# A copy block moved ahead of two others on ScalarE, and weight conversions begun earlier, in a three-stage attention and MLP-mixer kernel

## The chip, the cores and the metric

The kernel runs on one core of a Trainium2 chip. The metric is the device time of one execution in microseconds (us), as the median of three runs. TensorE is called PE here, VectorE DVE, ScalarE ACT, GpSimd POOL, and SyncE SP; SP issues the DMAs of this kernel.

## The reference

Local attention with a few global columns, then two token/channel mixers. Cut to what matters:

```python
x = attention(q, k, v)                      # B=2, S=768, E=512
# first mixer
u = x + (relu(x^T @ w_tok1) @ w_tok2)^T
u = u + relu(u @ w_ch1) @ w_ch2             # w_ch1: 512 x 1536
# second mixer (moe2)
theta = x @ w_theta
zr, zi = x * cos(theta), x * sin(theta)
yr = einsum('ts,bsd->btd', w_tok_r, zr)
yi = einsum('ts,bsd->btd', w_tok_i, zi)
u = x + yr + yi
out = u + relu(u @ w_ch)
```

The weights are 64-bit floats. The kernel keeps each operand of these products as two float32r halves, a high one (the rounded value) and a low one (the rest), and multiplies three pairs of halves for each product (`mm3`: high by high, high by low, low by high, in this order).

## The kernel before

Everything is written out in order by hand; each engine works through its own queue of instructions in that order, and semaphores hold an instruction until its inputs are there. There are three parts: the attention, the channel product of the first mixer (`channel_mix`, two batches b of twelve chunks k each), and the second mixer (`PhaseB.run`).

**The late steps.** `PhaseB.run` loops over twelve blocks i of 128 rows. In step i PE does `mix(i, 0)` (24 products y <- z and wri, 256 columns), `theta(i + 2)` (12 products th), and `mix(i, 1)` and `mix(i, 2)` (12 products of 512 columns each). What the other engines do in step i serves later blocks:

- `rotate(i + 1)`: DVE multiplies x by sine and by cosine (line 1170, two instructions), ACT copies each result as the high half of z (line 1171), POOL subtracts to get the low halves (line 1173, two instructions) and adds the two halves of xt to get x again (line 1177). `mix(i + 1, 0)` needs both. The high halves are read by its first product, the low half of the cosine part by its third. z has two buffers, named s and z in the trace: even blocks are in s, odd blocks in z.
- `turn_in(i + 3)`: the block i + 3 was turned by a DMA a step earlier, as 16-bit halves in the tile cut_xt. ACT joins the halves (line 789), ACT copies the high half of xt (line 792), DVE subtracts to get the low half (line 793).
- `turn_out(i + 4)`: ACT cuts the next block into 16-bit halves (line 779) in the same tile cut_xt, and SP issues the DMA that turns it.
- `theta(i + 2)`: after the products th, DVE reduces the angle (lines 1139, 1142, 1143, 1146, 1147), and ACT takes one absolute value and two sines (lines 1150 to 1152) that `rotate(i + 2)` needs one step later.
- `tick`, twice in steps 0 to 3 and once in the others: the conversion of weight pieces from 64-bit words to two float32r halves. A piece passes four phases in four successive ticks: two ACT instructions (lines 139, 140), then DVE, DVE and POOL (lines 145, 148, 149), then ACT (line 157), then DVE (line 160). Each tick moves every piece that is under way on by one phase and then begins one new piece, if its gate is open. A gate is a number that a counter has to reach; the counter goes up once for each chunk of the second batch. `need` adds ticks where a piece is not yet done.

In the first batch of `channel_mix` there is a tick after each of the two halves h of a chunk, in the second batch only after h = 1, and one more after the chunk's second product for most k.

Of the kernel before, what the change touches and what calls it, by code (L numbers as in the profile page):

```python
# [20 lines left out]
ALU = mybir.AluOpType  # L21
# [43 lines left out]
def r(ap):  # L65
    return ap.bitcast(F32R)
# [17 lines left out]
class Build:  # L84
# [851 lines left out]
    def moe_jobs(self, ws, w12p):  # L936

        dram = self.dram
        self.start_jobs()
        self.wc_job, self.wr_job = {}, {}  # L940
        self.wt, self.wr, self.wch = [], [], []
        self.ws, self.w12p = ws, w12p

        for i in range(2 * NF):
            self.wc_job[divmod(i, 2)] = 0 if i < self.EARLY else self.channel_job(*divmod(i, 2))

        def theta(d):
            if d == 0:
                self.s0 = self.xs_rows(0, self.xs_raw(0, "s0"))
                self.s1_raw = self.xs_raw(1, "s1")  # L950
                self.s1 = self.xs_rows(1, self.s1_raw)
                for i in range(NE):
                    t = self.s0 if i < 3 else self.s1
                    j = 2 * (i % 3)
                    self.wt.append((t[:, j], t[:, j + 1]))
            return self.wt[d]

        for d in range(NE):
            self.wt_job = self.add_job(
                dram["w_theta"][d * P : (d + 1) * P, :], lambda d=d: theta(d), 1  # L960
            )

        def token(i):
            if i < self.EARLY:
                w = self.early.tile([P, 2, E], F32, name="wri%d" % i, tag="w")
            else:
                w = self.split_tile(i - self.EARLY, "wri%d" % i, True)
            self.wr.append((w[:, 0], w[:, 1]))
            return self.wr[i]

        for i in range(3 * NS):
            s, j = divmod(i, 3)
            self.wr_job[s] = self.add_job(
                dram["w_tok"][s * P : (s + 1) * P, 2 * j * E : 2 * (j + 1) * E],
                lambda i=i: token(i),
                2 + i // 2,
            )

        def last(d):
            if d == 0:  # L980
                raw = w12p.tile([P, NS * 2 * E + W12_PAD], F32, name="wch", tag="w")
                w = raw[:, 0 : NS * 2 * E].rearrange("p (a l e) -> p a l e", a=NS, l=2)
                self.wch = [(w[:, i, 0], w[:, i, 1]) for i in range(NE)]
                self.wch_rest = w[:, NE:NS].rearrange("p a l e -> p (a l) e")
                self.wch_late = raw[:, NE * 2 * E + SHIFT : NS * 2 * E + SHIFT]
            return self.wch[d]

        for d in range(NE):
            self.wch_job = self.add_job(
                dram["w_ch"][d * P : (d + 1) * P, :], lambda d=d: last(d), 1 + NF  # L990
            )
# [28 lines left out]
    def channel_mix(self, gp, pb):  # L1020
        nc = self.nc
        steps = [(b, k) for b in range(B) for k in range(NF)]
        ho = {}

        def up(b, k):
            self.need(self.wc_job[k, 0])
            c1 = self.wc[k][0]
            uth, utl = self.ut[b]
            g = gp.tile([P, 2, S], F32R, name="g_%d_%d" % (b, k), tag="g")
            for h, hs in enumerate((slice(0, E), slice(E, S))):  # L1030
                ps = self.ps.tile([P, hs.stop - hs.start], F32, name="gp_%d_%d_%d" % (b, k, h), tag="t")
                self.mm3(
                    ps,
                    [
                        ((r(c1[0][:, d]), r(c1[1][:, d])), (r(uth[h][:, d]), r(utl[h][:, d])))
                        for d in range(NE)
                    ],
                )
                self.evac_split(g[:, 0, hs], g[:, 1, hs], ps, relu=True)
                if b == 0 or h == 1:  # L1040
                    self.tick()
            return g

        def down(b, k, g):
            self.need(self.wc_job[k, 1])
            c2 = self.wc[k][1]
            if k == 0:
                ho[b] = [
                    self.ps.tile([P, E], F32, name="h2_%d_%d" % (b, s), tag="acc") for s in range(NS)
                ]  # L1050
            for s in range(NS):
                cs = slice(s * P, (s + 1) * P)
                self.mm3(
                    ho[b][s],
                    [((g[:, 0, cs], g[:, 1, cs]), (r(c2[0]), r(c2[1])))],
                    first=k == 0,
                    last=k == NF - 1,
                )
                if k == NF - 1:
                    x = self.x[b][:, s, :]  # L1060
                    nc.vector.tensor_tensor(out=x, in0=ho[b][s], in1=x, op=ALU.add)  # L1061

        g = up(*steps[0])
        self.turning = {}
        plan = {2: [(pb.turn_out, 0)], 3: [(pb.turn_in, 0), (pb.turn_out, 1)], 4: [(pb.turn_in, 1)],
                5: [(pb.theta, 0)], 6: [(pb.rotate, 0), (pb.turn_out, 2)], 7: [(pb.theta, 1)],
                8: [(pb.turn_in, 2)], 9: [(pb.turn_out, 3)]}
        for i, (b, k) in enumerate(steps):
            nxt = up(*steps[i + 1]) if i + 1 < len(steps) else None
            if b == 0:  # L1070
                if 0 <= k - 4 < NS:
                    self.columns_split(k - 4)
                if 0 <= k - 3 < NS:
                    self.halves_join(self.turning[k - 3], nc.gpsimd.tensor_copy)
                if 0 <= k - 2 < NS:
                    self.columns_out(pb, k - 2)
            if b == 1:
                for act, n in plan.get(k, ()):
                    act(n)
            down(b, k, g)  # L1080
            if b == 1 and k < NF - 1 and k not in (5, 6, 7):
                self.tick()
            if (b, k) == (0, NF - 2) or b == 1:
                self.gate += 1
            g = nxt
        pb.run()


class PhaseB:
# [21 lines left out]
    def turn_in(self, i):  # L1111

        K = self.k
        j = (2, 1, 0)[i % 3] if i > 2 else i % 2
        if j not in self.xtile:
            pool, tag = (self.tp, "t") if j == 2 else (self.xtp, "xt%d" % j)
            self.xtile[j] = pool.tile([P, 2, NE, P], F32, name="xt%d" % j, tag=tag)
        t = self.xt[i] = self.xtile[j]
        K.halves_join(self.cut, K.nc.scalar.copy)
        K.halves_split(self.cut, r(t[:, 0]), r(t[:, 1]))  # L1120

    def theta(self, i):
        K, nc = self.k, self.k.nc
# [151 lines left out]
    def run(self):  # L1275
        K = self.k
        n = len(self.todo)
        TA, TB = self.TA, self.TB
        ends = []
        for b in range(B):  # L1280
            ends += [(b, 0, (0, 1), 0, TB), (b, 0, (2, 3), 0, TB)]
            ends += [(b, 1, (d,), 0, TA) for d in range(NE)]
        ends[-1:] = [(1, 1, (NE - 1,), c, c + TB) for c in range(0, TA, TB)]
        for i, (b, s) in enumerate(self.todo):
            self.mix(i, 0)
            if i + 1 < n:
                self.rotate(i + 1)
            if i + 3 < n:
                self.turn_in(i + 3)
            if i + 4 < n:  # L1290
                self.turn_out(i + 4)
            if i + 2 < n:
                self.theta(i + 2)
            if b == 1 and s in (0, NS - 1):
                self.last_split(s // (NS - 1), 0)
            self.mix(i, 1)
            if b == 1 and s > 0:
                self.last(*ends[s - 1])
            if b == 1 and s == 2:
                self.last_split(0, 1)  # L1300
            K.tick()
            self.mix(i, 2)
            if i < 4:
                K.tick()
        self.last_split(1, 1)
        for end in ends[NS - 1 :]:
            self.last(*end)
# [54 lines left out]
```

## Time and profile before

| what | value |
|---|---|
| time, median of 3 runs | 497.35 us (497.07 to 498.65) |
| the profiled execution's own time | 497.5 us |
| its span, first to last instruction | 495.7 us |
| PE busy | 486.2 us (98%) |
| DVE, ACT, POOL busy | 312.6, 264.8, 180.8 us |
| mean granted clock of PE | 0.996 |

The span is what the profile divides up; the execution's own time is 1.8 us longer. A granted clock of 1.00 is PE's upper level (2.4 GHz), 0.50 the lower one (1.2 GHz).

### The profile page before, as it was taken

The page shows a single profiled execution, that of the slowest core. Times are in us where ns is not written, and L with a number is a line of the kernel's source. Part 1 is how long each engine was busy: PE and PEld are TensorE (multiplying, and loading weights), DVE is VectorE, ACT ScalarE, POOL GpSimd, SP SyncE. Part 2 cuts the span into 40 slices and gives each one's busy share as a digit, 9 for nine tenths or more (in the row PEclk, how much of TensorE's full clock was granted, in tenths as well). Part 3 has the DMA queues.
Part 4 walks back from the last instruction along what each step waited for, and adds up shares of the span by engine and source line. Part 5 has one row for each costly group of instructions (what it writes and reads, how often), then busy time and mean ns, then how long its engine had stood idle before and what let it go on. Part 6 is the DMA issues. An engine that isn't in the chain of part 4 may idle for free.

```text
span 495.7 us, 7653 instructions
## 1 busy us (share of the span) xinstructions
PE 486.2 (98%) x2836; PEld 413.8 (83%) x2836; DVE 312.6 (63%) x671; ACT 264.8 (53%) x482; POOL 180.8 (36%) x187
## 2 busy tenths in 40 slices
PE   8999999999999999999999999999997999999997
PEld 5788878787888888888888888888886889888896
DVE  4688878845767698416466564676877675651442
ACT  6788778723655555213577546647665655432010
POOL 7445443420343666301333151354444453333000
PEclk9999999999999999999999999999998999999999
DMA  7787764302454545202445131514410001100012
GB/s 201 207 254 244 246 217 125 105 2 82 134 171 101 157 123 154 64 1 71 117 131 181 53 105 44 150 42 107 106 22 22 22 22 22 42 22 22 22 66 104
DMA packets 49022, 50.66 MB, mean 102 GB/s; under 512 B 20944, under 2 KB 39888, under 8 KB 48976
## 3 DMA queue, kind: packets, MB, share of 16 engines
q1 hardware_dynamic: 48976, 50.08, 34.8%
q8 instruction: 25, 0.41, 0.4%
q14 instruction: 21, 0.17, 0.1%
HBM read 42.21 MB, written 3.15 MB: 91 GB/s over the span
## 4 chain that ended last, share of the span: by engine, by line
PE 84%; DVE 7%; ACT 4%; DMA 2%; POOL 1%; SPq 1%; issue 1%; DVEq 0%; ACTq 0%; POOLq 0%
PE gp L96 20%; PE h L96 18%; PE y L96 14%; PE v L96 7%; PE mm L96 7%; PE o L406 6%; PE th L96 5%; PE t L484 4%; PE s L437 4%; DMA k<-k 1%; DVE w L1170 1%; DMA q<-q 1%; DVE cvs L145 1%; DVE xt L793 1%; DVE x L1061 1%
## 5 line engine op out<-in xcount | busy, mean ns | idle before, releaser
L149 POOL TENSOR_TENSOR cvt<-cvt,cvs 128x512 int32<-128x512 int32 (+1 forms) x57 | 75.5, 1325 | 189.9 <-DVE cvt L148 168.2
L96 PE MATMUL h<-wc,g 128*128 128x512 f32 x432 | 101.7, 389 | 0.0
L96 PE MATMUL gp<-xh,wc 128*128 128x512 f32 (+1 forms) x384 | 97.1, 335 | 0.0
L96 PEld LDWEIGHTS h<-wc,g 128*128 128x128 f32 x432 | 79.6, 188 | 15.2
L96 PEld LDWEIGHTS gp<-xh,wc 128*128 128x128 f32 x384 | 67.3, 189 | 8.6 <-DVE g L708 0.2
L708 DVE SCALAR_TENSOR_TENSOR g<-gp,g 128x512 fp32r<-128x512 f32 (+1 forms) x48 | 26.7, 556 | 64.7 <-ACT g L706 64.5
L96 PE MATMUL gp<-xl,wc 128*128 128x512 f32 (+1 forms) x192 | 64.3, 335 | 0.0
L96 PE MATMUL y<-wri,s 128*128 128x256 f32 (+1 forms) x288 | 53.7, 344 | 2.7 <-ACT s L1171 1.5
L96 PEld LDWEIGHTS y<-wri,s 128*128 128x128 f32 x288 | 46.2, 196 | 9.2 <-ACT s L1171 1.9
L96 PE MATMUL y<-wri,z 128*128 128x256 f32 (+1 forms) x288 | 52.0, 335 | 0.0
L706 ACT ACTIVATE g<-gp 128x512 fp32r<-128x512 f32 (+1 forms) x48 | 23.4, 487 | 52.7 <-PE gp L96 52.7
L96 PEld LDWEIGHTS y<-wri,z 128*128 128x128 f32 x288 | 44.6, 188 | 6.1 <-POOL z L1173 0.2
L484 PE MATMUL t<-ident,e 128*128 128x128 f32 x176 | 48.1, 285 | 0.4 <-ACT at L496 0.4
L145 DVE SCALAR_TENSOR_TENSOR cvs<-cvt,cvs 128x512 int32<-128x512 int32 (+1 forms) x57 | 44.8, 787 | 0.0
L96 PEld LDWEIGHTS gp<-xl,wc 128*128 128x128 f32 x192 | 36.1, 188 | 4.6
L484 PEld LDWEIGHTS t<-ident,e 128*128 128x128 f32 x176 | 31.7, 184 | 8.1 <-issue 2.0
L450 DVE CUSTOM_DVE_ANT_0 e<-s,base 128x256 f32<-128x256 f32 (+1 forms) x96 | 32.9, 397 | 8.7 <-PE s L437 7.3
L139 ACT ACTIVATE cvt<-raw 128x512 f32<-128x512 f32 (+1 forms) x57 | 37.2, 652 | 2.2 <-issue 2.2
L140 ACT ACTIVATE cvs<-raw 128x512 int32<-128x512 uint16 (+1 forms) x57 | 37.2, 653 | 0.0
L96 PE MATMUL th<-s,xt 128*128 128x512 f32 x144 | 35.0, 392 | 0.0
L406 PE MATMUL o<-v,at 128*128 128x65 f32 x192 | 32.3, 252 | 0.0
L96 PEld LDWEIGHTS th<-s,xt 128*128 128x128 f32 x144 | 26.3, 189 | 5.2 <-DVE g L708 0.4
(111 smaller groups left out, 817.2 us busy)
## 6 DMA issues: line engine op xcount, KB each, us to landing
raw<-w_ch SPq DMA_DIRECT2D x28, 512.0 KB, 4.2
raw<-w_tok SPq DMA_DIRECT2D x21, 512.0 KB, 4.1
k<-k SPq DMA_DIRECT2D x7, 480.0 KB, 5.8
v<-v SPq DMA_DIRECT2D x8, 384.0 KB, 3.9
out<-o SPq DMA_DIRECT2D x11, 256.0 KB, 2.1
q<-q SPq DMA_DIRECT2D x7, 384.0 KB, 5.0
raw<-w_theta SPq DMA_DIRECT2D x4, 512.0 KB, 4.0
a<-v SPq DMA_DIRECT2D x8, 240.0 KB, 4.6
```

The lines of the kernel that those rows point to most:

```text
L96: self.nc.tensor.matmul(out, lhsT=a, rhs=b, start=first and i == 0, stop=last and i == n - 1)
L139: nc.scalar.activation(out=f(t), in_=f(top), func=AF.Copy, scale=2.0**-111)
L140: nc.scalar.activation(out=s, in_=nxt, func=AF.Copy, scale=2.0**-13)
L145: nc.vector.scalar_tensor_tensor(out=s, in0=t, scalar=-(1 << 31), in1=s, op0=ALU.bitwise_and, op1=ALU.bitwise_or)
L149: nc.gpsimd.tensor_tensor(out=t, in0=t, in1=s, op=ALU.add)
L406: self.nc.tensor.matmul(po[:, j * OW : j * OW + D + 1], lhsT=at, rhs=v[:, j * (D + 1) : (j + 1) * (D + 1)], start=first, stop=last,)
L437: nc.tensor.matmul(ps[j][:, ii, c0:], lhsT=t["q"][pj, i * P : (i + 1) * P], rhs=kf[pj, i * KW - P + c0 : i * KW + P], start=True, stop=True,)
L450: nc.vector.tensor_tensor_reduce(out=e, in0=ps[j][:, ii, c0:], in1=self.base[2 * hp + j][min(i, 1)], op0=ALU.add, op1=ALU.min, scale=-SCAL ...
L484: nc.tensor.transpose(pt[:, ii, c, :], e[j][:, ii, c * P : (c + 1) * P], self.ident)
L706: nc.scalar.activation(out=hi, in_=ps, func=AF.Relu if relu else AF.Copy)
L708: nc.vector.scalar_tensor_tensor(out=lo, in0=ps, scalar=0.0, in1=f(hi), op0=ALU.max, op1=ALU.subtract)
L793: self.nc.vector.tensor_tensor(out=lo, in0=t[:, 1], in1=f(hi), op=ALU.subtract)
```

## The change

Four edits:

1. `turn_in` is split: the join and the high copy stay in it, and the subtraction on DVE becomes a function of its own, `turn_low`. In the plan of the second batch of `channel_mix` the two are called one behind the other, as before.
2. In `PhaseB.run` `turn_in(i + 3)` is called before `rotate(i + 1)` in steps 1 to 8, so ACT's join and high copy stand ahead of the rotation's two copies. `turn_low(i + 3)` stays behind the rotation. In step 0 the order is as it was.
3. In the second batch the chunks k = 0 and k = 1 have a tick after h = 0 as well.
4. The gates of the token weights' pieces i = 2, 4, 6, ... open one chunk earlier.

```diff
-                2 + i // 2,
+                max(2, 1 + (i + 1) // 2),
...
-                if b == 0 or h == 1:
+                if b == 0 or h == 1 or k < 2:
                     self.tick()
...
-        plan = {2: [(pb.turn_out, 0)], 3: [(pb.turn_in, 0), (pb.turn_out, 1)], 4: [(pb.turn_in, 1)],
+        plan = {2: [(pb.turn_out, 0)], 3: [(pb.turn_in, 0), (pb.turn_low, 0), (pb.turn_out, 1)],
+                4: [(pb.turn_in, 1), (pb.turn_low, 1)],
...
         K.halves_join(self.cut, K.nc.scalar.copy)
-        K.halves_split(self.cut, r(t[:, 0]), r(t[:, 1]))
+        K.nc.scalar.copy(out=r(t[:, 0]), in_=self.cut[:, 1])
+
+    def turn_low(self, i):
+        t = self.xt[i]
+        self.k.nc.vector.tensor_tensor(
+            out=r(t[:, 1]), in0=self.cut[:, 1], in1=t[:, 0], op=ALU.subtract
+        )
...
             self.mix(i, 0)
+            if 0 < i < n - 3:
+                self.turn_in(i + 3)
             if i + 1 < n:
                 self.rotate(i + 1)
+            if i == 0:
+                self.turn_in(3)
             if i + 3 < n:
-                self.turn_in(i + 3)
+                self.turn_low(i + 3)
```

ACT's queue in step 2 (it begins behind the last tick of step 1; z is the buffer of block 3, cut_xt_5 the turned block 5, w_3 the sines of block 3), before:

```order
L140 ACTIVATE cvs_9549<-raw_9445 128x512
L1171 CAST z_9362<-w_3_9497 128x512 x2
L789 COPY cut_xt_5_9481<-cut_xt_5_9481 128x2x512
L792 CAST xt_8732<-cut_xt_5_9481 128x512
L779 COPY cut_xt_0_9588<-x_66 128x1024
```

and after (the copies of the rotation now have line 1178, the high copy line 1121):

```order
L140 ACTIVATE cvs_9537<-raw_9433 128x512
L789 COPY cut_xt_5_9493<-cut_xt_5_9493 128x2x512
L1121 CAST xt_8744<-cut_xt_5_9493 128x512
L1178 CAST z_9374<-w_3_9509 128x512 x2
L779 COPY cut_xt_0_9598<-x_66 128x1024
```

Join and high copy have moved ahead of the two copies of the rotation; DVE's and POOL's queues have the same order in this place as before.

ACT's queue at the end of step 2 and the start of step 3 (wch are the last weights; s is the buffer of block 4), before:

```order
L157 ACTIVATE wch<-cvt_9548 128x512
L139 ACTIVATE cvt_9652<-raw_9552 128x512
L140 ACTIVATE cvs_9653<-raw_9552 128x512
L1171 CAST s_8532<-w_4_9604 128x512 x2
L789 COPY cut_xt_0_9588<-cut_xt_0_9588 128x2x512
```

and after:

```order
L157 ACTIVATE wch<-cvt_9560 128x512
L789 COPY cut_xt_0_9598<-cut_xt_0_9598 128x2x512
L1121 CAST xt_9382<-cut_xt_0_9598 128x512
L1178 CAST s_8493<-w_4_9614 128x512 x2
```

The last conversion that began there has begun earlier, so lines 139 and 140 are gone from this place. Of the conversions that began in the late steps this is the only one that has left them (six began there before, five now).

ACT's queue in chunks 0 and 1 of the second batch (g are the chunk's results, s the first weights of theta), before:

```order
L706 ACTIVATE g_0_8406<-gp_0_1_8422 128x256
L139 ACTIVATE cvt_8437<-raw_8154 128x512
L140 ACTIVATE cvs_8438<-raw_8154 128x512
L706 ACTIVATE g_1_8467<-gp_1_0_8468 128x512
L706 ACTIVATE g_1_8467<-gp_1_1_8483 128x256
```

and after:

```order
L706 ACTIVATE g_0_8406<-gp_0_1_8428 128x256
L139 ACTIVATE cvt_8446<-raw_8205 128x512
L140 ACTIVATE cvs_8447<-raw_8205 128x512
L706 ACTIVATE g_1_8476<-gp_1_0_8477 128x512
L157 ACTIVATE s_8492<-cvt_8422 128x512
L139 ACTIVATE cvt_8498<-raw_8426 128x512
L140 ACTIVATE cvs_8499<-raw_8426 128x512
L706 ACTIVATE g_1_8476<-gp_1_1_8504 128x256
```

Three ACT instructions of the conversions now stand between the two evictions (line 706) of chunk 1, and two more stand between those of chunk 0. PE's queue is the same throughout.

## Rows read from the trace of the kernel before

**Rows 1.** PE's waits in the whole span: us in total, times, longest us

```profile
PE y L96 <- ACT s L1171: 1.5, 1, 1.5
PE y L96 <- POOL s L1173: 1.2, 1, 1.2
```

**Rows 2.** Timeline of PE, late steps: start us, us, instruction, [idle before <-releaser]

```profile
349.63 2.99 PE L96 MATMUL y<-wri,s 128*128 128x256 f32 x24
...
352.46 2.88 PE L96 MATMUL th<-s,xt 128*128 128x512 f32 x12
...
360.62 3.15 PE L96 MATMUL y<-wri,z 128*128 128x256 f32 x24
...
366.34 5.60 PE L96 MATMUL y<-wri,z 128*128 128x512 f32 x24
373.46 0.50 PE L96 MATMUL y<-wri,s 128*128 128x256 f32 x2 [1.52 <-ACT s L1171]
375.17 4.38 PE L96 MATMUL y<-wri,s 128*128 128x256 f32 x22 [1.20 <-POOL s L1173]
379.38 2.93 PE L96 MATMUL th<-s,xt 128*128 128x512 f32 x12
...
387.58 2.99 PE L96 MATMUL y<-wri,z 128*128 128x256 f32 x24
```

**Rows 3.** Windows: stretch, us, busy us of each engine, PE's granted clock, DMA

```profile
22.00:24.00 2.00, 1.35 (x16) 1.10 (x15) 1.58 (x6) 2.00 (x5) 0.26 (x1) 1.00 0.26 83
...
376.00:377.00 1.00, 1.00 (x7) 1.00 (x6) 1.00 (x2) 0.06 (x1) 0.36 (x1) 0.50 0.04 8
```

**Rows 4.** Timeline of DVE, step 2 and the start of step 3

```profile
356.13 2.39 DVE L1170 TENSOR_TENSOR w<-x,w 128x512 f32<-128x512 f32 x2
...
361.19 1.53 DVE L793 TENSOR_TENSOR xt<-cut_xt,xt 128x512 fp32r<-128x512 f32 x1 [2.67 <-ACT xt L792]
...
363.36 0.43 DVE L1142 TENSOR_SCALAR w<-w 128x512 f32<-128x512 f32 x1
...
365.27 0.43 DVE L1147 TENSOR_SCALAR w<-w 128x512 f32<-128x512 f32 x1
...
370.38 2.38 DVE L1170 TENSOR_TENSOR w<-x,w 128x512 f32<-128x512 f32 x2
```

**Rows 5.** Timeline of ACT, start of step 2

```profile
356.02 0.65 ACT L140 ACTIVATE cvs<-raw 128x512 int32<-128x512 uint16 x1
...
358.55 0.62 ACT L1171 CAST z<-w 128x512 fp32r<-128x512 f32 x1 [1.03 <-DVE w L1170]
359.08 1.36 ACT L789 COPY cut_xt<-cut_xt 128x1024 uint16<-128x1024 uint16 x1
...
360.47 0.62 ACT L792 CAST xt<-cut_xt 128x512 fp32r<-128x512 f32 x1
```

**Rows 6.** Timeline of POOL, steps 2 and 3

```profile
356.36 1.61 POOL L149 TENSOR_TENSOR cvt<-cvt,cvs 128x512 int32<-128x512 int32 x1 [1.81 <-DVE cvt L148]
...
357.93 3.00 POOL L1173 TENSOR_TENSOR z<-w,z 128x512 fp32r<-128x512 f32 x2
...
360.90 1.27 POOL L1177 TENSOR_TENSOR x<-xt 128x512 f32<-128x512 f32 x1
...
372.17 2.94 POOL L1173 TENSOR_TENSOR s<-w,s 128x512 fp32r<-128x512 f32 x2
```

**Rows 7.** Timeline of DVE and POOL, step 4

```profile
387.40 0.69 DVE L793 TENSOR_TENSOR xt<-cut_xt,xt 128x512 fp32r<-128x512 f32 x1 [2.67 <-ACT xt L792]
387.48 1.78 POOL L1177 TENSOR_TENSOR x<-xt 128x512 f32<-128x512 f32 x1
...
388.73 0.81 DVE L1142 TENSOR_SCALAR w<-w 128x512 f32<-128x512 f32 x1
```

**Rows 8.** Timeline of PE and ACT, chunk 1 of the second batch

```profile
231.26 4.24 PE L96 MATMUL h<-wc,g 128*128 128x512 f32 x18
231.46 0.38 ACT L706 ACTIVATE g<-gp 128x256 fp32r<-128x256 f32 x1 [0.82 <-PE gp L96]
```

More of the change, by code (lines that the diff above doesn't have):

```diff
@@ L1064, in channel_mix @@
         self.turning = {}
-        plan = {2: [(pb.turn_out, 0)], 3: [(pb.turn_in, 0), (pb.turn_out, 1)], 4: [(pb.turn_in, 1)],
+        plan = {2: [(pb.turn_out, 0)], 3: [(pb.turn_in, 0), (pb.turn_low, 0), (pb.turn_out, 1)],
+                4: [(pb.turn_in, 1), (pb.turn_low, 1)],
                 5: [(pb.theta, 0)], 6: [(pb.rotate, 0), (pb.turn_out, 2)], 7: [(pb.theta, 1)],
-                8: [(pb.turn_in, 2)], 9: [(pb.turn_out, 3)]}
+                8: [(pb.turn_in, 2), (pb.turn_low, 2)], 9: [(pb.turn_out, 3)]}
         for i, (b, k) in enumerate(steps):
```

## The prediction, made before the changed kernel ran

> **What bounds the kernel now.** I read the page first: PE is busy for 98% of the span, so only its few gaps, and stretches at a low clock, can be won. The view of PE's waits lists them: the two long ones of the late steps are 1.5 and 1.2 us, each occurring once [rows 1]. The timeline of PE puts both into one place, the start of `mix(4, 0)` in step 4 [rows 2]. An undisturbed step takes 360.62 - 349.63 = 10.99 us, and its th products begin 352.46 - 349.63 = 2.83 us after its start. `mix(2, ·)` and `theta(4)` are like all others, and block 3's second part begins at 366.34; 24 products of 512 columns at the usual spacing last 5.44 us, since the same step shape gives 10.99 - 2.83 - 2.72 (the twelve th products are half of 24 such products, so the step's remaining 8.16 us are three times 2.72). So `mix(4, 0)` was due at 366.34 + 5.44 = 371.78 and its th at 374.61. They began at 379.38: **4.77 us lost**. The waits are 2.72 of it. Most of the rest is the clock: in the windows it is granted 0.50 behind the gap [rows 3], and 22 products took 4.38 us where 24 took 2.99 [rows 2]. Step 3 lost 0.16 too (3.15 against 2.99). Both together: 4.93.
>
> What is late is z of block 4. The timelines of the other engines say why. DVE comes back to the first multiplication of the rotation (line 1170) at 356.13 and 370.38, a **round of 14.25 us** against PE's 10.99 [rows 4]. The other engines fall 3.3 us further behind in each of steps 1, 2 and 3 until the lead is used up. From step 4 on there is one tick or none, and the round keeps up (block 5's mix begins on time at 387.58, 8.2 us after the th before it [rows 2]).
>
> Inside step 2, counted from line 1170's start at 356.13: DVE ends its two multiplications at +2.39; the second is held up by POOL, which ends line 149 at +1.84. ACT, free since +0.54, copies behind each multiplication (the second one from +2.42), joins from +2.95, copies the high half to +4.96 [rows 5]. DVE stands for 2.67 us until then, needs 1.53 for line 793 (to +6.59), and ends line 1147 at +9.57 [rows 4]. POOL subtracts from +1.80 to +4.80 [rows 6].
>
> **The change, part by part.** *ACT's order (steps 1 to 8).* Join and high copy need only the turned block, whose DMA was issued a step earlier. ACT starts them at +0.5 in place of idling for DVE: 1.36 to +1.85, 0.62 to +2.5. DVE's line 793 then follows its multiplications at once. The 2.67 us of standing go. Line 793 took 1.53 because POOL was in line 1177; alone it takes 0.69 [rows 7], so 0.84 more goes: 3.5 removed, and line 793 ends at +3.25.
>
> What it costs: the rotation's copies are now behind, to +3.1 and +3.7. POOL's two subtractions start at about +3.2 instead of +1.80, and meet DVE's angle work, which they had missed before. In step 4 such a meeting is on record: POOL's line 1177 took 1.78 with line 793 inside it, against 1.27 alone, and line 1142 took 0.81, ending just behind POOL, against 0.43 alone [rows 4, 6, 7]. I take it that DVE's lines 1142, 1146 and 1147 and POOL's instructions exclude each other. Then: line 1139 to +3.95; 1142 until POOL's first subtraction is over, +4.7; 1143 to +5.4; POOL's second subtraction to +5.9 (pushed back 0.2 by 1142); 1146 to +6.45; POOL's line 1177 to +7.7; 1147 to +8.0. Held up in all: 0.4 + 0.35 + 1.1 = 1.85. Line 1147 ends at +8.0 in place of +9.57, so **a round is 1.6 us shorter**, 12.65. The ticks behind it begin by that much earlier and are otherwise as before. The bounds of this term: 3.5 if nothing excludes anything, and -0.4 if DVE waits out all three POOL instructions (about 1.29 each, 3.9 against 3.5). I take 1.6, since the row of step 4 shows DVE waiting only for what is left of POOL's instruction.
>
> The Trainium skill has a rule here that speaks against the change: SBUF — State Buffer, section "Who interferes with whom", says that VectorE instructions with two SBUF inputs or in a 2-port mode and GpSimd instructions hold the pair exclusively, and that the later one "fully blocks". Read at its worst that is the -0.4 bound, a rival below; line 1143, with one input in PSUM, is free by that page. No row here shows 1143 beside POOL.
>
> *The sum for block 4.* Two shortened rounds (steps 1 and 2) bring line 1170 of step 3 from 370.38 to 367.2. z's last subtraction ends +5.9 behind it where ACT joins at +0.5. In step 3 ACT has two instructions fewer ahead of the join, because one conversion has left (below): some 1.1 us (two of 0.65, which overlap by 0.1), of which about 0.7 counts, since the first copy then waits for DVE again: +5.2. So z is ready at 372.4. PE's third product of `mix(4, 0)` needs it and is due at 371.78 - 0.16 + 0.24 = 371.9. **0.5 us remain of the wait, 1.2 without the conversion's part;** I take 0.6. In step 2, z of block 3 is ready at 356.13 - 1.6 + 5.9 = 360.4, ahead of its product (360.46 + 0.24), so the 0.16 goes. In step 4 z of block 5 is ready at about 367.2 + 11 + 4.7 = 382.9, where PE needs it at 371.6 + 0.6 + 10.99 + 0.24 = 383.4: just in time. Behind that the round is shorter than PE's step, as before.
>
> *The clock.* Near 23 us PE was idle for 0.65 of 2 us and the granted clock stayed at 1.00 [rows 3]; behind the gap of 2.72 it fell to 0.50. A wait of 0.6 is near the first, so I take no fall. The price if it falls is what it costs now: 4.38 for 22 products, where 22 of 24 parts of 2.99 are 2.74: 1.6.
>
> *The conversions in the first chunks (ticks and gates).* They move ACT, DVE and POOL work by one tick and add none. Their cost is the eviction of a chunk's second half, which stands behind up to three ACT instructions of some 0.65, 1.8 us later than 231.46 [rows 8]. It is hidden: PE spends 4.24 us on h before it starts the next chunk, and the first half of that goes into the other buffer. If the cover were gone it would cost 1.8 less that, nothing; I count 0. SP's loads move with the ticks, one ahead of a turning DMA in some places, which waits for ACT's line 779 anyway: 0. `turn_low` in the plan: same order, 0.
>
> *Sum:* 4.93 - 0.6 = 4.3 us won. The profiled execution took 497.5, 0.15 above the median, so 497.35 - 4.3 = **493.1 us**, 0.86% faster.
>
> **The rivals.**
> - *The wait goes altogether.* If POOL hinders DVE less than taken (nearer the bound 3.5), z is ready before 371.9 and all 4.93 come: 492.4. For it speaks that 1.85 is a sum of three meetings of which one is on record.
> - *A shorter gap still pulls the clock down.* A wait of 1.2 with a fall of 1.6 leaves 2.8 of the loss: 497.35 - 2.1 = 495.2. Whether a wait of that size does it, no row shows; the rows at 23 us speak against.
> - *POOL gives it all back (slower).* If DVE waits out each of the three POOL instructions, the round becomes 14.6 and line 1170 of step 3 starts at 371.1; z is ready at +5.2, 376.3. In the old order POOL ended at 372.17 + 2.94 = 375.1 [rows 6]. PE starts 1.2 later: 498.6, and some us more where block 3's wait pulls the clock down as well. It decides from 2.4 us held up per round in place of 1.85, plus what the later copies cost: two rounds must bring more than the 0.5 that z loses against line 1170 (5.2 against 4.73). Against it: POOL's three instructions are 3.9 us long and DVE has 1.8 us of work that needs no port among them.
> - *The edit does nothing*, because join or high copy must wait for the turned block or for the old xt. Against it: the block was turned a step earlier, and the old xt's last reader, POOL's line 1177, ends some 9 us before. 497.35.
>
> **How the numbers follow.** Forecast (492.8 to 494.2) 0.66; no wait 0.12, 492.4; clock falls 0.13, 495.2; given back 0.05, 498.6; nothing 0.04. A change of 0.3%, 1.5 us, is about what a measurement of this kernel can tell from none; faster means below 495.86. The first two cases and most of the third are: 0.66 + 0.12 + 0.10 = 0.88; the same: the rest of the third, the last, and some of the fourth, 0.08; slower 0.04. The range reaches from the no-wait case, 492.2, to the clock case with a wait of 1.5, 495.6; about 0.1 is left out.
>
> **What would show it.** After: no idle time before line 793's successor in steps 1 to 3 (`turn_low` directly behind line 1170's successor, 0.7 long); rounds of 12.4 to 13 us; POOL's subtractions starting +3.2 behind the round's start, and DVE's angle lines longer than 0.43 and 0.69; in PE's waits one entry of 0 to 1.2 us on POOL's z in place of 1.5 and 1.2; granted clock 1.00 in step 4; th of step 4 some 4.3 us earlier. Wrong would be a round still near 14 us, a clock of 0.50 behind a gap of under 1 us, or a new wait of PE in the first chunks of the second batch.

## The result, and the profile after

The changed kernel takes **493.03 us** (median of 4 runs, 492.38 to 493.48) against 497.32 us of the kernel before on the same chip: a ratio of 0.9907, 95% interval 0.9886 to 0.9929. The profiled execution's span fell from 495.7 to 491.5 us, 4.2 us.

PE's waits in the whole span, as in [rows 1] (us in total, times, longest us):

```profile
PE warm L330 <- DVE halfpi L228: 1.2, 1, 1.2
PE s L437 <- DMA q<-q: 0.8, 1, 0.8
PE s L437 <- DMA k<-k: 0.7, 1, 0.7
PE mm L96 <- ACT xh L706: 0.5, 1, 0.5
PE t L484 <- ACT at L496: 0.4, 1, 0.4
PE y L96 <- POOL s L1180: 0.2, 1, 0.2
```

The two waits of [rows 1] have become one of 0.2 us; the others stand in the attention and in the token products of the first mixer (mm), which the change doesn't touch. No line names the chunks of the second batch. The timeline of PE shows where the 0.2 stand; it answers to [rows 2]:

```profile
360.94 2.99 PE L96 MATMUL y<-wri,z 128*128 128x256 f32 x24
...
366.49 5.60 PE L96 MATMUL y<-wri,z 128*128 128x512 f32 x24
371.93 0.40 PE L96 MATMUL y<-wri,s 128*128 128x256 f32 x2
372.56 2.78 PE L96 MATMUL y<-wri,s 128*128 128x256 f32 x22 [0.24 <-POOL s L1180]
375.18 2.90 PE L96 MATMUL th<-s,xt 128*128 128x512 f32 x12
377.92 5.60 PE L96 MATMUL y<-wri,s 128*128 128x512 f32 x24
383.36 2.99 PE L96 MATMUL y<-wri,z 128*128 128x256 f32 x24
```

Block 3's mix is at its 2.99 us; block 4's starts on time, runs two products, waits 0.24 us for POOL's low half and goes on at full speed: 2.78 us for 22 products, where [rows 2] has 4.38. Its th begins at 375.18, 0.42 us later than an undisturbed step would have it (366.49 + 5.44 + 2.83 = 374.76), where it was 4.77 late before. The windows have PE's granted clock at 1.00 there (stretch, us, busy us of each engine, clock, DMA):

```profile
371.50:373.00 1.50, 1.26 (x8) 0.98 (x7) 1.43 (x3) 0.94 (x1) 1.50 (x2) 1.00 0.00 0
373.00:376.00 3.00, 3.00 (x25) 2.87 (x24) 2.49 (x4) 0.97 (x2) 0.94 (x1) 1.00 0.39 87
```

The timeline of DVE, ACT and POOL in step 2 and the start of step 3 answers to [rows 4 to 6]. The rotation's multiplications are now line 1177, ACT's copies 1178, POOL's subtractions 1180 and its addition 1184; the high copy of the turned block is 1121, DVE's subtraction 1125, the angle lines 1146 to 1154:

```profile
354.60 0.67 ACT L140 ACTIVATE cvs<-raw 128x512 int32<-128x512 uint16 x1
354.72 2.40 DVE L1177 TENSOR_TENSOR w<-x,w 128x512 f32<-128x512 f32 x2
...
355.17 1.36 ACT L789 COPY cut_xt<-cut_xt 128x1024 uint16<-128x1024 uint16 x1
356.56 0.62 ACT L1121 CAST xt<-cut_xt 128x512 fp32r<-128x512 f32 x1
357.09 1.14 ACT L1178 CAST z<-w 128x512 fp32r<-128x512 f32 x2
357.29 0.69 DVE L1125 TENSOR_TENSOR xt<-cut_xt,xt 128x512 fp32r<-128x512 f32 x1 [0.18 <-ACT xt L1121]
357.83 2.74 POOL L1180 TENSOR_TENSOR z<-w,z 128x512 fp32r<-128x512 f32 x2 [1.28 <-issue]
...
358.61 0.81 DVE L1149 TENSOR_SCALAR w<-w 128x512 f32<-128x512 f32 x1
359.46 0.69 DVE L1150 SCALAR_TENSOR_TENSOR w<-w,th 128x512 f32<-128x512 f32 x1
360.18 0.94 DVE L1153 SCALAR_TENSOR_TENSOR w<-w 128x512 f32<-128x512 f32 x1
360.54 1.73 POOL L1184 TENSOR_TENSOR x<-xt 128x512 f32<-128x512 f32 x1
361.16 1.40 DVE L1154 TENSOR_SCALAR w<-w 128x512 f32<-128x512 f32 x1
...
367.26 2.40 DVE L1177 TENSOR_TENSOR w<-x,w 128x512 f32<-128x512 f32 x2
...
369.23 3.28 POOL L1180 TENSOR_TENSOR s<-w,s 128x512 fp32r<-128x512 f32 x2
```

DVE stands 0.18 us where it stood 2.67, and its subtraction takes 0.69 in place of 1.53. In exchange lines 1149, 1153 and 1154 are 0.81, 0.94 and 1.40 long, since POOL's subtractions and addition now run beside them. A round is 367.26 - 354.72 = 12.54 us, 14.25 before.

The profiles can be compared more finely than the times. In the timelines of PE the last token products of the first mixer (mm, 36 of them) and block 1's mix begin here, in the kernel before and then in the changed one:

```profile
115.84 8.46 PE L96 MATMUL mm<-h,w 128*128 128x512 f32 x36 [0.66 <-ACT xh L706]
...
338.64 2.99 PE L96 MATMUL y<-wri,z 128*128 128x256 f32 x24
```

```profile
116.15 8.46 PE L96 MATMUL mm<-h,w 128*128 128x512 f32 x36 [0.54 <-ACT xh L706]
...
338.97 2.99 PE L96 MATMUL y<-wri,z 128*128 128x256 f32 x24
```

From the one to the other it is 222.80 and 222.82 us, and 222.80 to 222.82 in all eight profiles of this document: up to block 1's mix they differ only in what stood before mm, ahead of all edited code, and that scatters by 1.0 us (mm begins at 115.13 to 116.15). From the start of mm to the end of the span, without this scatter, the kernel before takes 495.7 - 115.84 = 379.9 us and the changed one 491.5 - 116.15 = 375.4: 4.5 us won. This part of the span is called the stretch from mm on below.

### The profile page after: what moved, and what is told of

Same layout as the page of the kernel before. It is cut to its first block, busy times and chain, and to the rows that moved or that the text cites. A ratio compares the mean times of both kernels' runs of the same rounds, so it can differ in the third digit from the quotient of the medians.

```text
span 491.5 us, 7645 instructions
## 1 busy us (share of the span) xinstructions
PE 484.3 (99%) x2836; PEld 412.3 (84%) x2836; DVE 317.4 (65%) x671; ACT 262.9 (53%) x482; POOL 180.8 (37%) x187
## 4 chain that ended last, share of the span: by engine, by line
PE 83%; DVE 5%; ACT 5%; POOL 3%; DMA 2%; issue 1%; DVEq 0%; SPq 0%; POOLq 0%; ACTq 0%
PE gp L96 20%; PE h L96 18%; PE y L96 13%; PE v L96 7%; PE mm L96 7%; PE o L406 5%; PE th L96 5%; PE t L484 4%; PE s L437 4%; DMA k<-k 2%; POOL base L319 1%; ACT cut_xt L789 1%; DVE x L1061 1%; DVE w L1154 1%; POOL s L1180 1%
## 5 line engine op out<-in xcount | busy, mean ns | idle before, releaser
L96 PE MATMUL y<-wri,s 128*128 128x256 f32 (+1 forms) x288 | 52.0, 335 | 0.2 <-POOL s L1180 0.2
L96 PEld LDWEIGHTS y<-wri,s 128*128 128x128 f32 x288 | 44.7, 189 | 6.4 <-POOL s L1180 0.4
L1157 ACT ACTIVATE w<-w 128x512 f32<-128x512 f32 x12 | 7.6, 632 | 49.4 <-DVE w L1154 49.4
```

Source lines behind the costliest of these rows:

```text
L96: self.nc.tensor.matmul(out, lhsT=a, rhs=b, start=first and i == 0, stop=last and i == n - 1)
L1157: nc.scalar.activation(out=a, in_=t, func=AF.Abs)
```

## The experiments

**The order alone.** Edits 1 and 2 without the ticks and gates:

```diff
-                max(2, 1 + (i + 1) // 2),
+                2 + i // 2,
...
-                if b == 0 or h == 1 or k < 2:
+                if b == 0 or h == 1:
                     self.tick()
```

> Edits 1 and 2 alone: join and high copy ahead of the rotation's copies, no extra ticks, gates as before. Theory (the order shortens the round, the conversion that left is worth 0.7 us in step 3): rounds of 12.5 us as with the whole change, z of block 4 ready +5.9 behind the start of its round in place of +5.3, a wait of 0.9 to 1.3 us of PE before the third product of mix(4, 0). If the granted clock stays at 1.00 behind it, 493.6 to 494.0 us; if it falls, some 495.3. Rival (the conversions carry the gain): rounds near 14.2 us and a time near 497.3.

Measured: 492.91 us (5 runs, 492.56 to 493.17) against 497.04 of the kernel before (15 runs), ratio 0.9913 (0.9899 to 0.9926). The wait and the rounds, from the waits of PE and the timelines of DVE and POOL:

```profile
PE y L96 <- POOL s L1180: 0.8, 1, 0.8
```

```profile
353.70 2.40 DVE L1177 TENSOR_TENSOR w<-x,w 128x512 f32<-128x512 f32 x2
...
366.22 2.39 DVE L1177 TENSOR_TENSOR w<-x,w 128x512 f32<-128x512 f32 x2
...
369.35 2.72 POOL L1180 TENSOR_TENSOR s<-w,s 128x512 fp32r<-128x512 f32 x2 [1.29 <-issue]
```

The round is 12.52 us, the same as with the whole change. z of block 4 is ready 369.35 + 2.72 - 366.22 = 5.85 us behind the round's start, in place of 369.23 + 3.28 - 367.26 = 5.25, and PE waits 0.83 us in place of 0.24. The granted clock stayed at 1.00. So the conversions are worth 0.6 us of waiting, and as much in the stretch from mm on (376.0 against 375.4 us), but nothing that the times can tell: the intervals of the two versions lie over each other. The wait is a little under what was expected (0.9 to 1.3 us), and the time 0.7 us under its range (493.6 to 494.0).

**The conversions alone.** Edits 3 and 4 on the kernel before (the same two lines, the other way round):

```diff
-                2 + i // 2,
+                max(2, 1 + (i + 1) // 2),
...
-                if b == 0 or h == 1:
+                if b == 0 or h == 1 or k < 2:
                     self.tick()
```

> Edits 3 and 4 alone on the kernel before: the two extra ticks and the earlier gates, the old order on ACT. Theory: rounds stay at 14.25 us, since ACT's two instructions that have left step 2 only lengthen its idle time before the rotation's copies; both waits of block 4 stay (1.5 and 1.2 us), the clock falls to 0.50, time 497.0 to 497.6. No new wait of PE in the first chunks of the second batch. Rival (the conversions carry part of the gain by themselves): a wait shorter by 0.7 us or more and a time of 496.5 or less.

Measured: 497.04 us (11 runs, 496.02 to 498.81) against 497.04, ratio 0.9997 (0.9985 to 1.0009): no gain and no cost. PE's waits:

```profile
PE y L96 <- ACT s L1171: 1.5, 1, 1.5
PE y L96 <- POOL s L1173: 1.2, 1, 1.2
...
PE y L96 <- POOL z L1173: 0.7, 1, 0.7
```

Both old waits are there to the tenth, and PE has no wait in the first chunks, which are busy throughout (25.00 of 25 us from 215 to 240 in the windows). One thing was not expected. In this profile the granted clock stayed at 1.00 behind the same gap, and then a third wait, 0.75 us, appeared at the start of block 5's mix. In its timeline of PE the products behind the second wait run at full speed:

```profile
374.95 2.78 PE L96 MATMUL y<-wri,s 128*128 128x256 f32 x22 [1.21 <-POOL s L1173]
377.56 2.90 PE L96 MATMUL th<-s,xt 128*128 128x512 f32 x12
380.30 5.60 PE L96 MATMUL y<-wri,s 128*128 128x512 f32 x24
385.74 0.40 PE L96 MATMUL y<-wri,z 128*128 128x256 f32 x2
386.88 2.86 PE L96 MATMUL y<-wri,z 128*128 128x256 f32 x22 [0.75 <-POOL z L1173]
```

So in the kernel before, the low clock hid a wait that stands behind it: block 5's z also came too late for a PE at full speed. The stretch from mm on is 379.3 us against 379.9, so the fallen clock cost 0.6 us on balance there, not 1.6.

**POOL's addition taken away.** The changed kernel, in which the rotations of blocks 2, 3 and 4 don't restore x:

```diff
-        nc.gpsimd.tensor_tensor(out=x, in0=whole(xt[:, 0]), in1=whole(xt[:, 1]), op=ALU.add)
+        if i not in (2, 3, 4):
+            nc.gpsimd.tensor_tensor(out=x, in0=whole(xt[:, 0]), in1=whole(xt[:, 1]), op=ALU.add)
```

> The changed kernel without POOL's addition that restores x in the rotations of blocks 2, 3 and 4 (x of these three blocks is left as it was, so this part of the output changes). It measures the price of POOL and DVE excluding each other. Theory: the last of DVE's angle instructions drops from 1.40 to 0.43 us in steps 1 and 2, and nothing else near it moves, so a round is about 1.0 us shorter (11.5 us), z of block 4 is ready 2 us earlier and no wait is left at mix(4, 0). Time at most 0.4 us under the changed kernel's, which one run can't tell. Rival (DVE's 1.40 has another cause than POOL's addition): it stays, and rounds stay at 12.5.

Measured: 492.1 us in one run. The timeline of DVE in steps 2 and 3:

```profile
353.00 2.39 DVE L1177 TENSOR_TENSOR w<-x,w 128x512 f32<-128x512 f32 x2
...
358.45 0.94 DVE L1153 SCALAR_TENSOR_TENSOR w<-w 128x512 f32<-128x512 f32 x1
359.43 0.43 DVE L1154 TENSOR_SCALAR w<-w 128x512 f32<-128x512 f32 x1
...
364.55 2.39 DVE L1177 TENSOR_TENSOR w<-x,w 128x512 f32<-128x512 f32 x2
```

Line 1154 is back at 0.43, while line 1153, which meets the subtractions, keeps its 0.94. The round is 364.55 - 353.00 = 11.55 us, 1.0 shorter, and PE has no wait for z at all: the stretch from mm on is 374.9 us, 5.0 under the kernel before, which is the whole loss of 4.93 that the prediction had counted. So the 1.40 was POOL's addition: the largest part of the price that the prediction had put on the new overlap is paid where it said.

**The other way to the same end.** ACT keeps the old order, and DVE moves its subtraction behind the angle work; the cut for the next block follows it (steps 1 to 8, conversions as in the changed kernel):

```diff
             self.mix(i, 0)
-            if 0 < i < n - 3:
-                self.turn_in(i + 3)
             if i + 1 < n:
                 self.rotate(i + 1)
-            if i == 0:
-                self.turn_in(3)
             if i + 3 < n:
-                self.turn_low(i + 3)
-            if i + 4 < n:
-                self.turn_out(i + 4)
+                self.turn_in(i + 3)
+            if i == 0:
+                self.turn_low(3)
+                self.turn_out(4)
             if i + 2 < n:
                 self.theta(i + 2)
+            if 0 < i < n - 3:
+                self.turn_low(i + 3)
+            if 0 < i < n - 4:
+                self.turn_out(i + 4)
```

> The old order on ACT (rotation's copies first, then join and high copy), but DVE does the angle work of theta before the subtraction of the turned block, and ACT's cut for the next block stands behind the sines; steps 1 to 8. Conversions as in the changed kernel. If what counts is that DVE no longer stands waiting for the high copy, this works as well: no idle time of 2.67 us on DVE, rounds of 12.2 to 12.9 us, POOL's subtractions back at +1.8 to +2.4, z ready at +5.0, wait at mix(4, 0) 0 to 0.3 us, time 492.6 to 493.2, the same as the changed kernel. Rival (the place of ACT's copies itself matters): rounds of 13.5 or more and a time of 495 or more.

Measured: 492.46 us (4 runs, 492.15 to 492.87), ratio 0.9902 (0.9887 to 0.9917): the same as the changed kernel. DVE in its timeline:

```profile
354.53 2.38 DVE L1177 TENSOR_TENSOR w<-x,w 128x512 f32<-128x512 f32 x2
...
361.42 0.68 DVE L1125 TENSOR_TENSOR xt<-cut_xt,xt 128x512 fp32r<-128x512 f32 x1
...
367.13 2.39 DVE L1177 TENSOR_TENSOR w<-x,w 128x512 f32<-128x512 f32 x2
```

No standing before the subtraction, a round of 12.60 us, and POOL's subtractions begin 1.80 us behind the round's start as in the kernel before. PE's waits list none on z, though block 4's mix takes 3.31 us in place of 2.99. What counts is that DVE doesn't stand waiting for the high copy; whether ACT hurries it or DVE does other work meanwhile makes no difference to the time.

**z of block 4 later, by one and by three POOL instructions.** The changed kernel with the first subtraction for this block repeated once, or three times (the same values written again; the second kernel has a 4 where this edit has the 2):

```diff
-        for c, w in ((1, t), (0, a)):
+        for c, w in ((1, t),) * (2 if i == 4 else 1) + ((0, a),):
             nc.gpsimd.tensor_tensor(out=r(z[:, c, 1]), in0=w, in1=z[:, c, 0], op=ALU.subtract)
```

> The changed kernel with POOL's first subtraction for block 4 done twice (the same values written again): z of this one block is late by one more POOL instruction, 1.27 us. Theory (z of block 4 is the only thing PE waits for here, and the next blocks have slack): PE's wait in mix(4, 0) grows from 0.24 to 1.5 us, block 5 shows a wait of at most 0.2, time 1.3 us above the changed kernel's, 494.1 to 494.6, if the granted clock stays at 1.00. Rival (a gap of this size costs more than itself, since the clock falls behind it): granted clock 0.50 in the products behind the wait and a time of 495 or more.

> The changed kernel with POOL's first subtraction for block 4 done four times in all: z of block 4 late by 3.8 us, so that PE's wait is longer than in the kernel before (4.0 against 2.72 us) while all else stays as changed. Theory: wait 4.0 us; if the clock falls as it did in the profile of the kernel before, some 1.6 us more in block 4's products, part of it hidden when block 5's z comes later too (POOL's and DVE's work of step 3 is late as well); time 497 to 498.5, back at the kernel before. Rival (the wait is worth only itself, the clock costs nothing on top): 496.8 or less and a granted clock of 1.00 in the profile.

Measured with one more: 494.01 us (4 runs, 493.85 to 494.34) against 497.24, ratio 0.9937 (0.9921 to 0.9954). With three more: 498.9 us (8 runs, 498.21 to 500.39), ratio 1.0035 (1.0023 to 1.0048). PE's timeline behind the wait, with one more:

```profile
373.13 2.78 PE L96 MATMUL y<-wri,s 128*128 128x256 f32 x22 [1.64 <-POOL s L1180]
...
383.93 2.99 PE L96 MATMUL y<-wri,z 128*128 128x256 f32 x24
```

and with three more, with the clock of the window behind it:

```profile
376.11 4.77 PE L96 MATMUL y<-wri,s 128*128 128x256 f32 x22 [4.72 <-POOL s L1180]
...
388.88 2.99 PE L96 MATMUL y<-wri,z 128*128 128x256 f32 x24
```

```profile
376.00:378.00 2.00, 1.89 (x9) 1.89 (x10) 1.18 (x2) 2.00 (x4) 1.75 (x2) 0.50 0.00 0
```

One more costs what it adds to the wait: 1.64 - 0.24 = 1.4 us, and 1.4 in the stretch from mm on (376.8 against 375.4 us). Between the medians, which come from different chips, it is 494.01 - 493.03 = 1.0, a little under the expected time. The clock stays up. Three more make the wait 4.72 us, the granted clock falls to 0.50, the 22 products take 2.0 us more, and the kernel is slower than the one before. Of the 6.5 us that come together (4.72 - 0.24 and 2.0) 6.4 show in the stretch from mm on (381.8 us) and 5.9 between the medians. The wait was longer than the 4.0 expected: each repetition took 1.5 us rather than 1.27. DVE's angle lines and one conversion line ran beside them, which is the likely reason; no run shows it. That put the time 0.4 above the expected 497 to 498.5.

## Why the prediction was right, point by point

*What bounds the kernel.* Right for the profile that it was read from: z of block 4. Moving that one tile by one POOL instruction lengthened the stretch from mm on by the added wait, and the three versions that only shortened the round to about 12.5 us (the change, the order alone, the other way) took 4.1 to 4.6 us off the medians. What the prediction didn't see is that in the old order z of block 5 is late as well when the clock stays up (the conversions alone, 0.75 us).

*ACT's order.* Right in the walk through a round, to within 0.2 us. Line 1125 ended at +3.26 where +3.25 was expected, line 1154 at +7.84 (expected +8.0), POOL's subtractions at +5.85 (+5.9). The round became 12.54 where 12.65 was worked out. The three lines of DVE were held up 0.38 + 0.25 + 0.97 = 1.6 us (1.85 expected), and 0.18 us of the standing stayed.

That POOL and DVE shut each other out was taken from one row of step 4; leaving the addition out has now shown it for the largest of the three meetings. For the two smaller ones no run leaves POOL's subtractions out: there it rests on the timeline. Line 1150, with one input in PSUM, keeps its 0.69 us inside POOL's subtractions. The Trainium skill (SBUF — State Buffer, section "Who interferes with whom") says that VectorE instructions with at most one SBUF input, outside the 2-port modes, do not contend with GpSimd, and the trace agrees. The worst case, a wait for the whole of POOL's instruction each time, did not come about: the three lines were held up 0.38, 0.25 and 0.97 us by instructions that last 1.27 to 1.30 alone. DVE came to each of them when it was already running, to the first subtraction for instance 358.61 - 357.83 = 0.78 us behind its start.

Two figures in the rival that gives it all back don't follow from its own terms. Two rounds bring more than 0.5 us as long as less than 3.5 - 0.25 = 3.25 us are held up in each, not 2.4; and DVE's lines with an input in PSUM, 1139 and 1143, are 0.68 + 0.69 = 1.4 us of work, not 1.8. With 1.6 measured the rival is out by either. The ends of the range, by the same terms, are 492.4 and 495.5, not 492.2 and 495.6.

*The conversions.* Right as a mechanism, 0.6 us of waiting (0.7 expected). By themselves they do nothing. They are free in the first chunks, as the equal 222.8 us with and without them show. The eviction that they delay was sized too high: in chunk 1 it starts 0.92 us behind the start of h, where it was 0.20 in [rows 8], so 0.7 us later and not 1.8 (PE and ACT after the change):

```profile
231.58 4.24 PE L96 MATMUL h<-wc,g 128*128 128x512 f32 x18
...
232.50 0.37 ACT L706 ACTIVATE g<-gp 128x256 fp32r<-128x256 f32 x1
```

*The sum for block 4.* z was ready at 372.51 (372.4 expected), and the wait was 0.24 where 0.6 was taken. All engines entered the late steps 0.33 us later in this profile (`mix(1, 0)` begins at 338.97, against 349.63 - 10.99 = 338.64), so against PE z came 0.2 us earlier than worked out: each of the two rounds was 0.1 shorter. 4.93 - 0.42 = 4.5, which is what the stretch from mm on lost; less the 0.33, which come from before mm, it is the 4.2 of the span. By cause, z of block 4 came 2.9 us earlier against PE (two rounds, each 1.7 shorter, less 0.5 that it loses within the last one), and 1.6 came from the clock. That the median of the runs meets the forecast to 0.1 us is luck in part: the runs of the changed kernel alone lie 1.1 us apart.

*The clock.* Right that it would stay up behind a short wait; it did so behind 0.83 and 1.64 us as well, so the rival in which 1.2 us pull it down did not come about in these executions. One term was sized for one execution only: the 1.6 us that the clock took in the profile before. In the runs of the kernel before the mean granted clock of the execution was 1.00 in four of fifteen (496.66 to 497.40 us, median 496.96) and 0.993 to 0.997 in the others (496.89 to 498.49 us, median 497.22), so the fall mostly costs less than 1.6 us there. Three of them, at 0.993, took 498.0 us or more; no trace of such an execution was kept. The profile of the conversions alone, which has the old order on ACT, shows a reason for the smaller cost: with the clock up, block 5's z is the next to be late, by 0.75 us. That wait is gone with the new order as well (block 5's mix starts at 383.36 without one). In the stretch from mm on the changed kernel is 4.5 us shorter than the old order with the fallen clock and 3.9 shorter than the old order with the clock up (375.4 against 379.9 and 379.3 us). The sum's 4.3 lies between the two.

## What to carry to other kernels

When a pipeline's helper engines have a longer round than the engine they feed, the wait shows up only where the lead is used up; the step to mend is in every round ahead of it. The late input comes earlier by the number of rounds times what is saved in each, less what the new order costs within the last round (here 2.9 us), and the gain is cut off where the wait ends; a clock that fell behind the wait comes on top, less the waits that it hid. Look in the slow engine's timeline for the place where it stands for another engine's queue, and ask which of that engine's instructions could run earlier because their inputs have long been there, or what the waiting engine could do meanwhile. Then walk one round on paper with the new order, and count which instructions now meet on POOL and DVE: about half of the 3.3 us that the order won in each round here (2.5 of standing and 0.84 of line 793) was given back that way.

## What the runs showed of the hardware

The granted clock doesn't fall behind every such gap: behind 1.5 and 1.2 us of waiting it was 0.50 in the profile of the kernel before and 1.00 in that of the conversions alone, with nearly the same instructions around. Where it does fall, the time lost is smaller than the slow products suggest as long as the next input is late anyway, in these two profiles 1.6 us in block 4's products, 0.6 between the two stretches from mm on. Where nothing was late behind it, it was paid in full: with z of block 4 three POOL instructions later, block 5's mix starts without a wait, and 6.4 of the 6.5 us of waiting and slow products show in that stretch.

A VectorE instruction that meets a GpSimd instruction took longer here by part of it, not by all of it: line 1154 went from 0.43 to 1.40 us beside POOL's addition and back to 0.43 without it.
